# The projection's input rows cut as three tiles of 128 and a rest of 64, and the two products of u placed side by side

## Chip, cores and metric

The kernel runs on one core of one Trainium2 chip. The metric is the device time of one execution in microseconds (us); less is better. The kernel before took 781.15 us as the median of three runs (775.3 to 781.82).

## What is computed

One sequence `u` of 2048 rows and 448 channels goes through two branches, and a gate per row mixes them:

```python
g = sigmoid((x * gate_w).sum(-1, keepdims=True))
a = A(x)          # long convolution per channel by FFT, kernel K from log_A_real, A_imag, C, log_dt; plus u * D_skip
b = B(x)          # q, k, v = x @ wq, x @ wk, x @ wv; 16 heads of 28; four segments of 512 rows:
                  # causal softmax inside the segment, and a memory M, z of all earlier segments; then @ wo
return g * a + (1 - g) * b
```

The change touches the three projections `x @ wq`, `x @ wk`, `x @ wv` (448 inputs each) and the first transform of `u`'s FFT.

## The kernel before

**Split products.** q, k and v need nearly full fp32 accuracy, and the kernel gets it from single-pass products (type fp32r) of split operands: `x = xh + xl`, `w = wh + wl`, and `x w = xh wh + xh wl + xl wh`. The 448 inputs lie as four tiles of 112 partitions, so one output takes 4 x 3 = 12 products, accumulated in one PSUM bank. `matmuls` (L784) does that for a unit, that is one of 4 segments, one group of 4 heads, q or k: 12 products of 112 x 128 weights with 512 columns; there are 32 units. `values` (L857) does it for v and the gate's sum: 12 products of 450 columns for each of 16 blocks of 128 rows.

**Making the parts.** For each block of 128 rows of u, four transposes (L899) bring 4 x 112 channels onto partitions in one PSUM bank; `copy(xh, pv)` (L905) rounds them, and one subtraction on VectorE (L906) leaves `xl`. The weights of q and k are split once and stored to DRAM (`WD`, L769), 448 KB for each group of heads and matrix, and loaded again for every unit (L780, one unit ahead). The weights of v are split by `rest` (L742) and stay.

**u's transform.** `transform_u` (L541) makes the first step of u's FFT: 16 loads of u with 64 rows on the upper and 64 on the lower half of the partitions, and for each half one fp32 product of 64 rows, 128 outputs and 448 columns (each is two instructions in the trace), copied out of PSUM (`gs`) and stored (`GU`). It yields after each of the 32 products.

**The first half's order.** `first_half` (L312) makes the convolution kernel K in 56 items `n`, four to a group; each item needs three passes of ScalarE (`cs`) over 128 x 1024, four VectorE products (L409 to L415) and 64 small products on TensorE (`sums`, tile `ps_k`); between groups `decays` makes six exponentials. Into this sequence `Feed` (L493) mixes the projection, step by step: each step yields a cost, a positive or negative number of us, and `spend` (L511) gives each item an allowance, `ITEMS[n % 4] * RATES[n // 4]`, and each place in `decays` one of `PLACE`; steps are issued until the allowance is used up, what is over or short is carried on, and a negative cost ends the turn. A yield of `"pe"` after each pair of units holds the feed until the next exponentials (`exps`, L519), so that ScalarE doesn't change its table more often.

**The filler.** u's products are the filler. `project` takes two at both sides of `remember()` in its light stretches (L952, L955) and one at the start of segments 1 to 3 (L891). `spend` takes one more when the feed is held and over 1.5 us of allowance are left (L516). What is left of the 32 is issued around the last items: `fill(2)` (L477), `fill(4, False)` (L482) and `rest` (L533).

**Queues.** TensorE takes its products in the order of the program (`mm`, L1521). In the main loop ScalarE's activations and copies are chained in program order, too (`follow`, L1472). Products of projection, memory and u all write PSUM tiles `ps_m`, of which there are three (L1647). Of a pair of units both tiles are kept until the exponentials, copies and subtractions that follow the hold have read them (L960 to L967). `transform_k` (L570) and the attention follow, with other PSUM tiles and the whole of `kb`, which L436 fills after the last `sums`.

Of the kernel before, what the change touches and what calls it, by code (L numbers as in the profile page):

```python
# [12 lines left out]
F32 = mybir.dt.float32  # L13
# [298 lines left out]
def first_half(nc, k, gy, feed):  # L312
# [228 lines left out]
def transform_u(nc, k, up, pp):  # L541

    uv = k.u.rearrange("(n h w) d -> h n w d", h=2, w=16)
    guv = k.GU.rearrange("k r (h w) d -> h (k r) w d", h=2)
    def load(w):
        ut = up.tile([128, D], F32, tag="ut", name="ut", bufs=3)
        for h in range(2):
            nc.sync.dma_start(ut[64 * h : 64 * h + 64], uv[h, :, w])
        return ut

    uts = {0: load(0), 1: load(1)}
    for w in range(16):
        if w < 14:
            uts[w + 2] = load(w + 2)
        ut = uts.pop(w)
        for h in range(2):
            pt = k.ps("m")
            k.mm(
                pt[:, :D], k.s1u[64 * h : 64 * h + 64], ut[64 * h : 64 * h + 64],
                start=True, stop=True,  # L560
            )

            where, tag, bufs = (pp, "xin", 4) if w >= 12 and h else (up, "gs", 3)
            gs = where.tile([128, D], F32, tag=tag, name="gs", bufs=bufs)
            k.copy(gs, pt[:, :D], AF.Copy)
            nc.sync.dma_start(guv[h, :, w], gs)
            yield 0.9
# [156 lines left out]
def project(nc, k, pp, early, filling):  # L724

    act, copy, v = k.act, k.copy, nc.vector
    gw = pp.tile([112, 4, 2], F32, name="gw")
    nc.gpsimd.memset(gw, 0.0)
    nc.sync.dma_start(gw[:, :, 0], k.gate_w.rearrange("(k p) -> p k", p=112))
    wvh = pp.tile([112, 4, 450], F32R, name="wvh")  # L730
    wvl = pp.tile([112, 4, 450], F32R, name="wvl")
# [6 lines left out]
    nid = early.tile([112, 112], F32R, name="nid")  # L738
    with k.issue_after(k.chained):
        v.tensor_scalar(nid, k.ident[:112, :112], -1.0, None, ALU.mult)  # L740

    def rest(lo, x, hi):  # L742

        pt = k.ps("m")[:112, : x.shape[-1]]
        k.mm(pt, k.ident[:112, :112], x, start=True, stop=False)
        k.mm(pt, nid, hi, start=False, stop=True)
        copy(lo, pt, AF.Copy)

    wsp = [pp.tile([112, 4, 2, 4, 32], F32R, name=f"wsp{i}") for i in range(2)]
# [3 lines left out]
    def weights():  # L753
        for kt in range(4):
            t = pp.tile([112, D], F32, tag="xin", name="winv", bufs=4)
            nc.sync.dma_start(t, k.wv[112 * kt : 112 * kt + 112])
            for x, n in ((gw[:, kt], slice(448, 450)), (t, slice(0, D))):
                copy(wvh[:, kt, n], x, AF.Copy)
                rest(wvl[:, kt, n], x, wvh[:, kt, n])
            yield 0.3  # L760
        for i, src in enumerate((k.wq, k.wk)):
            for kt in range(4):
                t = pp.tile([112, D], F32, tag="xin", name="win", bufs=4)
                (k.bulk if i else nc.sync.dma_start)(t, src[112 * kt : 112 * kt + 112])
# [10 lines left out]
    def load_w(u):  # L775
# [3 lines left out]
        w = pp.tile([112, 4, 2, 128], F32R, tag="w", name="w", bufs=2)  # L779
# [4 lines left out]
    def matmuls(u, x):  # L784
# [3 lines left out]
        n = 0  # L788
# [68 lines left out]
    def values(s, xh, xl, ts):  # L857
        for t in ts:
            pt = k.ps("m")
            n = 0  # L860
            for kt in range(4):
                for a, b in ((xh, wvh), (xh, wvl), (xl, wvh)):
                    k.mm(
                        pt[:, :450], a[:, kt, 128 * t : 128 * t + 128], b[:, kt],
                        start=(n == 0), stop=(n == 11),
                    )
                    n += 1
                if kt == 1:
# [19 lines left out]
    for s in range(NSEG):  # L888
# [3 lines left out]
        xh = pp.tile([112, 4, SEG], F32R, tag="xh", name="xh")  # L892
        xl = pp.tile([112, 4, SEG], F32R, tag="xl", name="xl")
        for t in range(4):
# [4 lines left out]
            for kt in range(4):  # L899
                k.tr(  # L900
                    pt[:112, 128 * kt : 128 * kt + 128], xin[:, 112 * kt : 112 * kt + 112], k.ident
                )
# [3 lines left out]
            v.tensor_tensor(xl[:, :, ts_], pv, xh[:, :, ts_], ALU.subtract)  # L906
# [36 lines left out]
        for i in range(0, len(units), 2):  # L943
# [6 lines left out]
            for u in us:  # L950
                if pts:
                    for _ in range(2 if light else 0):  # L952
                        yield -next(filling, 0.1)
                    yield from remember()
                    for _ in range(2 if light else 0):  # L955
# [3 lines left out]
                yield 0.65  # L959
# [506 lines left out]
def gated_mix(ctx, tc, k):  # L1466
# [110 lines left out]
    k.WD = dr.tile([2, 4, 112, 4, 2, 128], F32, name="WD")  # L1577
# [182 lines left out]
```

## Time and profile before

| | |
|---|---|
| median of the three runs | 781.15 us |
| the profiled execution: its own time | 780.51 us |
| its span, first to last instruction | 778.7 us (1.8 us lie outside) |
| busy: TensorE (PE) / VectorE (DVE) / ScalarE (ACT) | 681.5 / 560.4 / 502.7 us |
| mean granted TensorE clock | 0.967 |
| first half (to the last `sums`) | about 0 to 419 us |
| DMA, mean over the span | 203 GB/s |

A row of the timeline gives start, duration, engine, line, operation, output <- inputs, the shape as rows*columns of the weights and the moving tile, and how many instructions are merged; in brackets stands how long the engine was idle before, and what ended that. Matmuls are pipelined: a product's duration overlaps the next one's, and what it costs on TensorE is the distance from its start to the next start. All TensorE products share one line (L1522), so they are told apart by their tiles. In a table of windows each row gives the stretch, its length, and for each engine its busy time and number of instructions, then granted clock, DMA share and GB/s. A row of a group gives count | busy time, mean ns of one | idle time before.

### The profile page before, as it was taken

Reading aid. Unit: us, or ns where it says so; the run is one execution under the profiler, and the core shown is the slowest. Engines: PE = TensorE matmul, PEld = TensorE weight load, DVE = VectorE, ACT = ScalarE, POOL = GpSimd, SP = SyncE. Lnnn points to the kernel's source line nnn. Section 1 sums busy time; section 2 is a strip of 40 time slices with the busy share of each in tenths; the row PEclk is TensorE's granted clock in tenths of the full one; section 3 lists DMA queues with packets and bytes.
Section 4 is the critical chain, followed back from the end, with each engine's and each line's share of the span. In section 5 each row is a group of like instructions: output and inputs, shape, how many; then the busy total and the mean of one; then the engine's idle time right before and its main releaser. Section 6 shows DMA issues by size and latency. Waiting matters only on the chain.

```text
span 778.7 us, 19775 instructions
## 1 busy us (share of the span) xinstructions
PE 681.5 (88%) x8273; PEld 371.0 (48%) x8289; DVE 560.4 (72%) x758; ACT 502.7 (65%) x621; POOL 157.9 (20%) x193
## 2 busy tenths in 40 slices
PE   1685998999988998889999999898899789979897
PEld 1362555666555665457664444343334334434333
DVE  8989679878899788888875345565555675674486
ACT  4877689889999989988986425665435353451220
POOL 5405300110111101110120002343311221132110
PEclk9998999999999999999999989999999899999899
DMA  9428774234563345733356797999676867556686
GB/s 242 127 71 247 231 250 131 70 106 161 156 219 111 108 126 168 231 130 105 117 211 237 283 323 274 324 333 338 230 233 207 305 208 244 195 195 242 171 266 191
DMA packets 91550, 158.00 MB, mean 203 GB/s; under 512 B 22174, under 2 KB 59542, under 8 KB 91462
## 3 DMA queue, kind: packets, MB, share of 16 engines
q1 hardware_dynamic: 85530, 153.55, 59.9%
q10 hardware_dynamic: 5052, 2.33, 1.2%
q8 instruction: 65, 1.06, 0.6%
q0 software_dynamic: 880, 0.87, 0.4%
q14 instruction: 23, 0.19, 0.1%
HBM read 88.51 MB, written 60.24 MB: 191 GB/s over the span
## 4 chain that ended last, share of the span: by engine, by line
PE 53%; ACT 18%; DVE 14%; DMA 8%; issue 4%; SPq 1%; POOL 1%; ACTq 0%; DVEq 0%; POOLq 0%
PE ps_m L1522 23%; PE ps_c L1522 8%; ACT cs L1476 6%; PE ps_w L1522 5%; PE ps_pv L1522 5%; PE ps_arg L1522 4%; PE ps_mx L1522 4%; PE ps_k L1522 4%; ACT EY L1476 2%; DVE pr L1476 2%; DVE mx L1476 2%; DMA WD<-wsp 1%; DVE xl L906 1%; ACT L1476 1%; DMA V<-VD 1%
## 5 line engine op out<-in xcount | busy, mean ns | idle before, releaser
L1476 DVE TENSOR_REDUCE mx<-ps_mx 128x2 f32<-128x1024 f32 (+3 forms) x128 | 102.4, 821 | 96.2 <-PE ps_mx L1522 93.1
L1476 ACT ACTIVATE PT<-ps_w 128x1024 f32<-128x1024 f32 (+1 forms) x96 | 84.5, 881 | 128.5 <-PE ps_w L1522 119.4
L366 POOL TENSOR_TENSOR EX<-EX,cab 128x1024 f32<-128x1024 f32 x28 | 53.5, 1913 | 288.2 <-ACT EX L1476 266.6
L1476 ACT ACTIVATE cs<-ps_arg 128x1024 f32<-128x1024 f32 x97 | 94.5, 1023 | 3.7 <-DVE Y L414 2.4
L1522 PE MATMUL ps_w<-qu,ku 32*128 32x512 f32 (+3 forms) x768 | 89.5, 350 | 4.6 <-ACT PT L1476 3.3
L1098 POOL TENSOR_SCALAR_AFFINE_SELECT PT<-PT 128x256 f32<-128x256 f32 (+1 forms) x96 | 47.4, 494 | 227.0 <-ACT PT L1476 219.6
L1522 PE MATMUL ps_m<-xh,w 112*128 112x512 f32 x256 | 91.4, 410 | 1.3 <-DMA w<-WD 1.3
L1522 PEld LDWEIGHTS ps_w<-qu,ku 32*128 32x128 f32 x768 | 58.6, 189 | 68.0 <-ACT PT L1476 30.7
L409 DVE TENSOR_TENSOR X<-EX,cs 128x1024 f32<-128x1024 f32 x56 | 69.3, 1238 | 12.6 <-ACT cs L1476 11.8
L1522 PE MATMUL ps_k<-Y,X 128*32 128x64 f32 x3584 | 64.1, 226 | 14.4 <-DVE Y L414 14.4
L1522 PEld LDWEIGHTS ps_k<-Y,X 128*32 128x32 f32 x3584 | 54.9, 113 | 40.4 <-DVE Y L414 22.4
L413 DVE TENSOR_TENSOR Y<-EY,cs 128x1024 f32<-128x1024 f32 x56 | 70.1, 1253 | 0.0
L1476 ACT ACTIVATE cs<-cs 128x1024 f32<-128x1024 f32 x56 | 59.2, 1057 | 1.3
L1522 PEld LDWEIGHTS ps_m<-xh,w 112*128 112x128 f32 x256 | 48.1, 188 | 21.1 <-issue 8.3
L1476 ACT ACTIVATE EY<-ps_arg 128x1024 f32<-128x1024 f32 x52 | 51.3, 1036 | 3.9 <-PE ps_arg L1522 3.7
L1522 PE MATMUL ps_arg<-ct,lh 64*128 64x512 bf16 x224 | 46.4, 384 | 7.0 <-ACT EY L1476 4.9
L1522 PE MATMUL ps_m<-xl,w 112*128 112x512 f32 x128 | 50.3, 393 | 0.0
L1522 PE MATMUL ps_pv<-PT,V 128*32 128x128 f32 (+3 forms) x512 | 46.4, 461 | 4.4 <-DMA V<-VD 4.4
L1522 PEld LDWEIGHTS <-lh 64*128 64x128 bf16 x392 | 20.2, 94 | 59.0 <-issue 46.5
L1522 PE MATMUL ps_m<-wo,pvs 128*128 128x448 f32 x96 | 43.9, 589 | 1.4 <-ACT mn L1476 1.1
L1522 PE MATMUL ps_mx<-ku,qu 32*128 32x512 f32 (+3 forms) x256 | 44.4, 379 | 0.3 <-DMA ku<-KD 0.3
L415 DVE SCALAR_TENSOR_TENSOR Y<-EY,cs 128x512 f32<-128x512 f32 x56 | 40.0, 715 | 3.8 <-ACT cs L1476 2.5
(219 smaller groups left out, 1284.0 us busy)
## 6 DMA issues: line engine op xcount, KB each, us to landing
w<-WD SPq DMA_DIRECT2D x32, 448.0 KB
qu<-QD SPq DMA_DIRECT2D x16, 512.0 KB
ku<-KD SPq DMA_DIRECT2D x16, 512.0 KB
GU<-gs SPq DMA_DIRECT2D x32, 224.0 KB
GK<-gs SPq DMA_DIRECT2D x8, 896.0 KB
gk<-GK SPq DMA_DIRECT2D x16, 448.0 KB
gu<-GU SPq DMA_DIRECT2D x16, 448.0 KB
ks<-ks SPq DMA_DIRECT2D x32, 224.0 KB
```

The costliest lines, as they stand in the source:

```text
L366: nc.gpsimd.tensor_tensor(o, o, cab, ALU.mult)
L409: v.tensor_tensor(X, ex, t[:, :, 0], ALU.mult)
L413: v.tensor_tensor(Y[:, :, :, :32], lo, y[:, :, :, ::-1], ALU.mult)
L415: v.scalar_tensor_tensor(Y[:, 1, :, 32:], ey[:, :, 32:], -1.0, y[:, 1], ALU.mult, ALU.mult)
L906: v.tensor_tensor(xl[:, :, ts_], pv, xh[:, :, ts_], ALU.subtract)
L1098: nc.gpsimd.affine_select(sl, sl, pat, ALU.is_ge, 0.0, base=0, channel_multiplier=-1)
L1476: x = op(*args, **kw)
L1522: tc.keep_in_program_order(nc.tensor.matmul(*args, **kw))
```

## The change

- The 448 inputs are cut as 128 + 128 + 128 + 64. The first three tiles take three products each. The fourth tile holds both parts: rows 64 to 127 the rounded channels 384 to 447, rows 0 to 63 what the rounding left of them, and the weights of these channels twice. One product of 128 rows then gives `xh wh + xl wh`, and one product of the upper 64 rows gives `xh wl`: 11 products instead of 12.
- `xl` has three tiles; the subtraction is two instructions, one of 128 x 384 and one from the upper to the lower 64 partitions of 128 columns.
- `WD` and its tiles have 128 partitions instead of 112 (512 KB a load instead of 448); the rest of each weight matrix and of `gate_w` is loaded twice, by two DMAs.
- u's two products of a load stand next to each other, with `tile_position` given; then come both copies and stores, and one yield of 1.7 instead of two of 0.9. The filler has 16 pairs instead of 32 products; `fill(1)`, `fill(2, False)` and one step instead of two in the light stretches take the same number of products at these places.
- A unit's last step costs the feed 0.45 instead of 0.65, a block of v 1.0 instead of 1.2. `RATES`, `ITEMS` and `PLACE` stay.

```diff
@@ first_half
-            feed.fill(2)
+            feed.fill(1)
...
-    feed.fill(4, False)
+    feed.fill(2, False)
@@ transform_u
-        for h in range(2):
-            pt = k.ps("m")
+        pts = [k.ps("m") for _ in range(2)]
+        for h, pt in enumerate(pts):
             k.mm(
                 pt[:, :D], k.s1u[64 * h : 64 * h + 64], ut[64 * h : 64 * h + 64],
-                start=True, stop=True,
+                start=True, stop=True, tile_position=(64 * h, 0),
             )
-
+        for h, pt in enumerate(pts):
             where, tag, bufs = (pp, "xin", 4) if w >= 12 and h else (up, "gs", 3)
             gs = where.tile([128, D], F32, tag=tag, name="gs", bufs=bufs)
             k.copy(gs, pt[:, :D], AF.Copy)
             nc.sync.dma_start(guv[h, :, w], gs)
-            yield 0.9
+        yield 1.7
@@ project
+    def terms(x, w):
+        xh, xl = x
+        wh, wl = w
+        for kt in range(3):
+            yield xh[:, kt], wh[:, kt]
+            yield xh[:, kt], wl[:, kt]
+            yield xl[:, kt], wh[:, kt]
+        yield xh[:, 3], wh[:, 3]
+        yield xh[64:, 3], wl[64:, 3]
@@ matmuls
-        for kt in range(4):
-            for a, b in ((0, 0), (0, 1), (1, 0)):
-                k.mm(pt, w[:, kt, a], x[b][:, kt], start=(n == 0), stop=(n == 11))
-                n += 1
-            if kt < 3:
+        for n, (a, b) in enumerate(terms(x, (w[:, :, 0], w[:, :, 1]))):
+            k.mm(pt, b, a, start=(n == 0), stop=(n == 10))
+            if n in (2, 5, 8):
                 yield 0.65
@@ values: the same, with n == 5 for the yield inside a block, and at its end
-            yield 1.2
+            yield 1.0
@@ the parts of x
-            for kt in range(4):
-                k.tr(
-                    pt[:112, 128 * kt : 128 * kt + 128], xin[:, 112 * kt : 112 * kt + 112], k.ident
-                )
-            pv = pt[:112].rearrange("p (k q) -> p k q", k=4)
+            for kt, c in enumerate((0, 128, 256, 320)):
+                k.tr(pt[:, 128 * kt : 128 * kt + 128], xin[:, c : c + 128], k.ident)
+            pv = pt.rearrange("p (k q) -> p k q", k=4)
             ts_ = slice(128 * t, 128 * t + 128)
             copy(xh[:, :, ts_], pv, AF.Copy)
-            v.tensor_tensor(xl[:, :, ts_], pv, xh[:, :, ts_], ALU.subtract)
+            v.tensor_tensor(xl[:, :, ts_], pv[:, :3], xh[:, :3, ts_], ALU.subtract)
+            v.tensor_tensor(xh[:64, 3, ts_], pv[64:, 3], xh[64:, 3, ts_], ALU.subtract)
@@ the units
-                    for _ in range(2 if light else 0):
+                    if light:
                         yield -next(filling, 0.1)
                     yield from remember()
-                    for _ in range(2 if light else 0):
+                    if light:
                         yield -next(filling, 0.1)
                 pts.append((yield from matmuls(u, x)))
                 load_w(after[u])
-                yield 0.65
+                yield 0.45
@@ DRAM
-    k.WD = dr.tile([2, 4, 112, 4, 2, 128], F32, name="WD")
+    k.WD = dr.tile([2, 4, 128, 4, 2, 128], F32, name="WD")
```

More of the change, by code (lines that the diff above doesn't have):

```diff
@@ L754, in weights @@
         for kt in range(4):
-            t = pp.tile([112, D], F32, tag="xin", name="winv", bufs=4)
-            nc.sync.dma_start(t, k.wv[112 * kt : 112 * kt + 112])
+            t = pp.tile([128, D], F32, tag="xin", name="winv", bufs=4)
+            rows(nc.sync.dma_start, t, k.wv, kt)
             for x, n in ((gw[:, kt], slice(448, 450)), (t, slice(0, D))):
@@ L859, in values @@
             pt = k.ps("m")
-            n = 0
-            for kt in range(4):
[L862 to L865, printed above, removed]
-                    )
-                    n += 1
-                if kt == 1:
+            for n, (a, b) in enumerate(terms((xh, xl), (wvh, wvl))):
+                k.mm(
+                    pt[:, :450], a[:, 128 * t : 128 * t + 128], b,
+                    start=(n == 0), stop=(n == 10),
+                )
+                if n == 5:
                     yield 1.2
```

39 lines of the change are left out of this document (22 added, 17 removed).

## The prediction

> **What bounds the kernel now.** I read the page first, then a table of windows cut at the first X product of each group of four items, then the timeline of single stretches, and the chain of waits last.
>
> ```profile
> span 778.7 us, 19775 instructions
> ```
>
> ```profile
> PE 53%; ACT 18%; DVE 14%; DMA 8%; issue 4%; SPq 1%; POOL 1%; ACTq 0%; DVEq 0%; POOLq 0%
> ```
>
> The chain is more than half TensorE, but everything that the change touches lies in the first half, and there the limit alternates:
>
> ```profile
> core 0: us, PE busy (x) PEld busy (x) DVE busy (x) ACT busy (x) POOL busy (x), PEclk, DMA share, GB/s
> 199.89:223.49 23.60, 21.64 (x347) 12.95 (x347) 21.73 (x29) 23.00 (x28) 3.82 (x2) 1.00 0.61 198
> 223.49:248.22 24.73, 20.78 (x354) 12.40 (x350) 23.90 (x35) 23.75 (x30) 3.83 (x2) 1.00 0.45 147
> 248.22:273.76 25.54, 25.01 (x362) 18.08 (x363) 20.86 (x30) 22.71 (x26) 3.83 (x2) 1.00 0.28 86
> 273.76:299.08 25.32, 23.91 (x353) 15.01 (x353) 21.01 (x29) 22.74 (x26) 3.82 (x2) 1.00 0.54 173
> 322.46:349.51 27.05, 23.10 (x359) 13.97 (x357) 24.25 (x33) 24.39 (x31) 3.83 (x2) 0.94 0.42 141
> ```
>
> Where v and the first units of a segment are made (248 to 299), TensorE is busy for 25.0 and 23.9 us and ScalarE idles 2.8 and 2.6 us. Where the light stretches with the filler lie (200 to 248), ScalarE is busy for 23.0 of 23.6 us, and TensorE has 2 to 4 us to spare. A TensorE saving counts in the first kind only; whatever ScalarE must do or wait for costs time in the second kind.
>
> **A unit and a block of v.** The timeline around one unit:
>
> ```profile
> 153.46 0.38 PE L1522 MATMUL ps_arg<-mag,one 64*128 64x512 bf16 x2
> ...
> 153.68 0.38 PE L1522 MATMUL ps_arg<-ct,lh 64*128 64x512 bf16 x2
> ...
> 153.99 0.50 PE L1522 MATMUL ps_m<-xh,w 112*128 112x512 f32 x1
> ...
> 154.33 0.40 PE L1522 MATMUL ps_m<-xl,w 112*128 112x512 f32 x1
> ...
> 156.42 0.39 PE L1522 MATMUL ps_m<-xl,w 112*128 112x512 f32 x1
> ...
> 156.66 0.39 PE L1522 MATMUL ps_m<-xh,w 112*128 112x512 f32 x1
> ...
> 156.97 1.10 PE L1522 MATMUL ps_k<-Y,X 128*32 128x64 f32 x64
> ```
>
> Starts inside the unit are 0.23 apart (156.42 to 156.66). Two products of 64 rows take 0.22 together (153.46 to 153.68), so one takes that long as well. A change of the rows and columns that a product occupies costs extra: 0.31 from the last 64-row pair to the unit (153.68 to 153.99, 0.09 more), 0.34 for the unit's first product (0.11 more), 0.31 for its last one before `ps_k` (0.08 more). The new unit has ten full products and a 64-row one at its end. So it saves two full products, 0.46, and pays 0.22 and one more change, 0.09: a gain of 0.15 where `ps_k` follows. Where `ps_arg` or u follows, the 64-row form is needed anyway: 0.24. Where a full product follows, the way there and back costs 0.22 + 0.08 + 0.09 + 0.11 = 0.50, a loss of 0.04. By the order of the timeline 17, 12 and 3 of the 32 units end so. For all units that is 5.3 us; about 16 of them lie where TensorE is the limit: **-2.6 us**.
>
> ```profile
> 164.66 0.37 PE L1522 MATMUL ps_m<-wvl,xh 112*128 112x450 f32 x1
> ...
> 164.87 0.37 PE L1522 MATMUL ps_m<-wvh,xl 112*128 112x450 f32 x1
> ```
>
> For v a product is 0.21. Of the twelve blocks of segments 1 to 3 seven end before `ps_arg` (gain 0.20 each), one before `ps_k` (0.11), four before a full product (loss 0.08): -1.2. The four of segment 0 end before full products: +0.3. Together **-0.9 us**.
>
> **The parts of x.** The subtraction becomes two.
>
> ```profile
> L409 DVE TENSOR_TENSOR X<-EX,cs 128x1024 f32<-128x1024 f32 x56 | 69.3, 1238 | 12.6 <-ACT cs L1476 11.8 <-DVE macc L851 0.3
> ...
> L414 DVE TENSOR_TENSOR Y<-EY,cs 128x512 f32<-128x512 f32 x56 | 39.3, 702 | 0.0
> ...
> L1476 ACT ACTIVATE gs<-ps_m 128x448 f32<-128x448 f32 x21 | 11.1, 540 | 7.0 <-PE ps_m L1522 7.0
> ...
> L906 DVE TENSOR_TENSOR xl<-ps_m,xh 112x512 fp32r<-112x512 f32 x16 | 10.3, 684 | 0.7 <-ACT xh L1476 0.7
> ```
>
> 1024 columns take 1.238, 512 take 0.702: 0.00105 a column and 0.166 fixed. At most the second instruction adds that fixed part to each of 16 subtractions, 2.7 us; at least nothing, where VectorE has room. Twelve lie in busy decays (23.90 us of 24.73): I take **+1.0**.
>
> **Weights.** Each load and store of `WD` is a seventh larger.
>
> ```profile
> 65.55 6.35 DMA WD<-wsp
> ...
> 77.90 3.97 DMA WD<-wsp
> ...
> 85.28 5.51 DMA w<-WD
> ```
>
> These 15.8 us of the chain of waits are exposed. If they grow with the bytes it is +2.3, if their time is latency 0; **+0.8**. The five extra small DMAs go through SP's queue before 60 us, under the parameters' VectorE work: 0, at most the 0.3 to 0.4 each that SP needs, 2 us.
>
> **u's pairs: where the feed puts them.** This is the term that decides. Costs fall by 0.2 per unit and block, allowances stay, so the feed reaches its hold earlier. Item 23 (allowance 2.5 x 1.12 = 2.80): before, it enters with 0.98, spends four steps of 0.65, and has 1.18 left at the hold, under the 1.5 of L516. After, item 22 already does three steps, item 23 enters with -0.57, spends 0.45, and is held with 1.78: it asks for filler. Going through all yields like this, filler in the hold is taken before at items 7 and 55 only; after at 7, 11, 19, 23, 27 and 35. So the last pair goes out at item 37, and none is left for the tail.
>
> In the hold both tiles of a pair of units are unread, and `ps_m` has three. A pair of u needs two, so the second product waits until ScalarE has copied the first out, on a queue behind the item's three `cs` passes; behind that product TensorE holds `sums` and the next exponents. Then ScalarE waits for the product. The tail of before shows such a turn:
>
> ```profile
> 416.69 0.62 DVE L1476 COPY gs<-ps_m 128x448 f32<-128x448 f32 x1
> ...
> 417.37 1.02 PE L1522 MATMUL ps_m<-ut,s1u 64*128 64x448 f32 x2 [0.31 <-DVE gs L1476]
> ...
> 418.32 1.10 PE L1522 MATMUL ps_k<-Y,X 128*32 128x64 f32 x64
> 418.47 0.54 ACT L1476 ACTIVATE gs<-ps_m 128x448 f32<-128x448 f32 x1 [0.83 <-PE ps_m L1522]
> ```
>
> The copy ends at 417.31, the product starts at 417.37, the next copy at 418.47: 1.16 us. With the copies, 2 x 0.54, ScalarE is held up 2.24 us a time. How full it is there:
>
> ```profile
> 207.88 1.94 ACT L1476 ACTIVATE cs<-ps_arg 128x1024 f32<-128x1024 f32 x2
> ...
> 209.85 1.06 ACT L1476 ACTIVATE cs<-cs 128x1024 f32<-128x1024 f32 x1
> ...
> 210.94 1.28 ACT L1476 ACT_TABLE_LOAD   x1
> ```
>
> At item 23 it goes from `cs` to the exponentials' table without a gap. Items 23 and 27 pay in full, 4.5; at 19 and 35 the same turn blocks TensorE (0.95 + 0.6 + 0.95) in groups that it limits, about 2 each; items 7 and 11 have slack, 0.5. Bounds: 0, if all lies in slack, and 6 x 2.24 = 13.4. I take **+9**.
>
> **What that frees.** The group at 322 loses three copies on ScalarE, -1.6. In the tail the product at 417.37 no longer stands ahead of the last `sums` (418.32), which sets `kb` and the second half: -1.0. Together **-2.6**. Elsewhere u's products side by side save TensorE time that is spare.
>
> **Sum.** -2.6 - 0.9 + 1.0 + 0.8 + 9 - 2.6 = +4.7 on the profiled execution's 780.5 (span 778.7 and 1.8 outside it): 785.2, rounded to **785 us**. The median of before, 781.15, is 0.6 above that execution, within its runs' spread.
>
> **Rivals.**
>
> *The waits in the hold are covered.* For it: a hold with 1.5 us left means that the item has less TensorE work than planned, and 273.76 to 299.08 shows ScalarE idle 2.6 us. Against it: no gap after 209.85. It replaces +9 by 0: **776**.
>
> *Two full products saved and no change paid, on a path that is TensorE all over.* A chain with 53% PE speaks for it: 32 x 0.23 + 16 x 0.21 = -10.7, with the pairs covered and -1.0 in the tail: **769**. Against it stand the 0.31 and 0.34 above and ScalarE's 23.00 of 23.60.
>
> *The clock falls in the new waits* (slower). With TensorE waiting behind a pair's first product, a stretch can look like the first of these:
>
> ```profile
> 133.20:136.60 3.40, 1.60 (x10) 0.59 (x7) 3.40 (x6) 3.40 (x6) 0.00 (x0) 1.00 0.73 257
> 136.60:140.00 3.40, 3.40 (x76) 3.03 (x75) 2.12 (x4) 1.77 (x3) 1.55 (x1) 0.50 0.64 202
> ...
> 228.10:231.50 3.40, 2.00 (x70) 1.20 (x66) 3.40 (x5) 3.37 (x6) 0.00 (x0) 1.00 0.42 124
> ```
>
> After 3.4 us with TensorE busy for 1.60, the granted clock is 0.50 for the next 3.4; with 2.00 busy it stayed at 1.00. That is the point from which it decides: an item with a hold and under about 1.8 us of TensorE work. A half-speed stretch does 1.7 us of work less; four of the six on the path are +6.8: **792**. [...]
>
> *The change doesn't do what it says*, if the 64-row product occupies the whole array. Then no change is paid, and each unit and block saves one full product net: for the 16 units and 16 blocks on the path 16 x 0.23 + 16 x 0.21 = 7.0 instead of my 3.5: **782**, hardly to be told from the forecast by time.
>
> **How the numbers follow.** Forecast (with the last rival) 0.50, covered waits 0.20, full saving 0.13, clock 0.17. About 1%, 7.8 us, is what a measurement of this kernel can tell from no change, that is 773 to 789. The full saving, and the lower part of the covered waits (with the subtraction and the weights at their lower bounds, 774, and the second half's order free to shift), are faster: 0.20. The clock, and the forecast with 13.4 for the waits (789.6) or both bounds of subtraction and weights, are slower: 0.32. The rest is 0.48. The range takes in the full saving at its end and the clock with the larger waits: 769 to 797. The forecast's own range is 776 to 793.
>
> **What would show it.** Right: no u product after about 370 us; in six places a `ut,s1u` pair with a `gs` copy between its two products, and ScalarE idle 0.6 to 1.2 us before the second copy; each unit 0.15 to 0.24 shorter; 0.3 around the 64-row product; last `sums` directly after its item. Wrong: the pairs in the hold start together; the groups at 200 to 248 not longer; or the second half, which the change doesn't touch, differing by more than a us or two.

## The result and the profile after

The changed kernel took **854.25 us** (median of four runs, 850.67 to 857.62) beside 781.09 for the kernel before on the same chip: a ratio of **1.095**, 95% interval 1.089 to 1.102. The forecast was 785, the range 769 to 797. A ratio below comes, like this one, from runs side by side; where disturbed runs are left out of it, it needn't be the quotient of the medians.

The profiled execution took 850.67 us, 70.2 more than that of before. The first and the last X product (items 0 and 55) cut both spans in three. The two rows are the answers for the line of the X product, before and after: count, durations, first and last start.

```profile
L409 DVE TENSOR_TENSOR X<-EX,cs x56: 1211/1221/2148, 63.0 to 413.8; 128x1024 f32<-128x1024 f32 x56
```

```profile
span 849.0 us, 19734 instructions
...
L409 DVE TENSOR_TENSOR X<-EX,cs x56: 1209/1218/2167, 65.3 to 446.0; 128x1024 f32<-128x1024 f32 x56
```

So 2.3 us are lost before item 0, 29.9 in the main loop (380.7 instead of 350.8), and **38.1 from the last X product to the end** (403.0 instead of 364.9), where nothing but the calls of the filler is changed.

**The tail and the second half.** Windows of after, then of before, with TensorE's busy time first and the granted clock third from the end:

```profile
443.53:446.94 3.41, 1.10 (x64) 0.94 (x64) 3.41 (x5) 3.36 (x4) 0.00 (x0) 1.00 0.44 160
446.94:450.36 3.42, 1.40 (x55) 1.41 (x59) 2.62 (x9) 0.39 (x3) 0.00 (x0) 0.50 0.00 0
480.00:500.00 20.00, 20.00 (x83) 8.10 (x81) 2.67 (x4) 4.58 (x5) 0.00 (x0) 0.50 0.26 107
```

```profile
412.96:416.38 3.42, 2.66 (x69) 1.80 (x70) 3.42 (x5) 2.59 (x5) 0.00 (x0) 1.00 0.47 144
416.38:419.79 3.41, 3.10 (x69) 1.53 (x68) 1.24 (x3) 1.13 (x3) 0.28 (x1) 1.00 0.85 314
```

Before, the filler of the tail keeps TensorE busy for 2.66 and 3.10 us of 3.4. With the change none is left; the `sums` alone are 1.10, and the next window runs at 0.50. It then stays there for 85 us, to 532.28, although TensorE is busy for 20.00 of 20 us in between. The timeline of that place in after:

```profile
445.48 1.10 PE L1536 MATMUL ps_k<-Y,X 128*32 128x64 f32 x64 [2.57 <-DVE Y L414]
448.96 1.93 PE L1536 MATMUL ps_k<-Y,X 128*32 128x64 f32 x64 [2.37 <-DVE Y L414]
452.13 3.36 PE L1536 MATMUL ps_w<-kb,s1k 32*128 32x448 f32 x8 [1.24 <-DVE kb L436]
```

Eight products of `transform_k` take 3.36 us; before they take 1.77 (at 420.68). So the products do run at the clock that the records show. The window before the fall wasn't idle: TensorE was busy for 1.10 of its 3.41 us. Nor did a busy TensorE bring the full clock back: from 452 to 529 us the distances between starts give about 62 us to products of 32 rows and 13 to products of 128, with 2.0 us of gaps, and the clock stayed at 0.50.

**The main loop.** TensorE's waits between 90 and 410 us, us in total, times, longest; after, then before:

```profile
PE ps_m L1539 <- DMA xin<-in_A_u: 3.9, 2, 2.3
PE ps_m L1536 <- ACT gs L1490: 3.8, 6, 0.6
PE ps_m L1536 <- DVE tm L872: 3.6, 3, 1.2
...
PE ps_m L1536 <- DVE lo L827: 2.3, 2, 2.1
PE ps_m L1536 <- DVE lo L829: 2.2, 1, 2.2
```

```profile
PE ps_m L1522 <- DVE macc L851: 0.4, 1, 0.4
```

Waits for `gs`, `tm` and `lo` are new, 11.9 us, and 11.7 of them stand ahead of products of u, which wait for a reader of a `ps_m` tile. New are also 3.9 us in which the transposes wait for the load of `xin`. One place of the first kind in after, a pair in the hold and the next one in the decay behind it:

```profile
251.85 1.02 PE L1536 MATMUL ps_m<-ut,s1u 64*128 64x448 f32 x2
...
252.90 0.54 ACT L1490 ACTIVATE gs<-ps_m 128x448 f32<-128x448 f32 x1 [2.65 <-PE ps_m L1536]
...
253.50 1.02 PE L1536 MATMUL ps_m<-ut,s1u 64*128 64x448 f32 x2 [0.63 <-ACT gs L1490]
...
254.55 0.55 ACT L1490 ACTIVATE gs<-ps_m 128x448 f32<-128x448 f32 x1 [1.11 <-PE ps_m L1536]
...
255.92 0.91 PE L1536 MATMUL ps_m<-ut,s1u 64*128 64x448 f32 x2
...
258.92 0.85 PE L1536 MATMUL ps_m<-ut,s1u 64*128 64x448 f32 x1 [2.08 <-DVE lo L827]
```

The first four rows are the turn that the prediction worked out. The last two aren't in it: the pair at 255.92, outside of the hold, needs its second tile while the units still keep theirs, and waits for VectorE's `lo`.

### The profile page after: what moved, and what is told of

The parts are those of the page before. It is cut to its first block, busy times and chain, and to the rows that moved or that the text cites. A ratio compares the mean times of both kernels' runs of the same rounds, so it can differ in the third digit from the quotient of the medians.

```text
span 849.0 us, 19734 instructions
## 1 busy us (share of the span) xinstructions
PE 727.8 (86%) x8224; PEld 377.3 (44%) x8241; DVE 566.7 (67%) x775; ACT 503.2 (59%) x620; POOL 156.4 (18%) x193
## 4 chain that ended last, share of the span: by engine, by line
PE 46%; DVE 14%; ACT 11%; DMA 7%; issue 3%; SPq 1%; DVEq 0%; ACTq 0%; POOL 0%
PE ps_m L1536 17%; PE ps_c L1536 8%; PE ps_w L1536 6%; PE ps_pv L1536 5%; PE ps_mx L1536 4%; PE ps_k L1536 3%; PE ps_arg L1536 3%; ACT cs L1490 2%; DMA ks<-ks 2%; DVE pr L1490 2%; DVE Y L413 2%; ACT L1490 2%; DVE X L409 1%; DVE pvs L1490 1%; ACT EY L1490 1%
## 5 line engine op out<-in xcount | busy, mean ns | idle before, releaser
L1536 PE MATMUL ps_w<-qu,ku 32*128 32x512 f32 (+3 forms) x768 | 91.7, 357 | 4.3 <-ACT PT L1490 3.9
L1536 PE MATMUL ps_m<-xh,w 128*128 128x512 f32 (+1 forms) x256 | 92.8, 433 | 1.6 <-DMA w<-WD 1.6
L1536 PEld LDWEIGHTS ps_w<-qu,ku 32*128 32x128 f32 x768 | 60.5, 195 | 67.8 <-ACT PT L1490 31.5
L1536 PE MATMUL ps_k<-Y,X 128*32 128x64 f32 x3584 | 68.5, 234 | 14.2 <-DVE Y L414 13.9
L409 DVE TENSOR_TENSOR X<-EX,cs 128x1024 f32<-128x1024 f32 x56 | 69.3, 1237 | 14.6 <-ACT cs L1490 12.5
L1536 PEld LDWEIGHTS ps_k<-Y,X 128*32 128x32 f32 x3584 | 58.7, 119 | 38.6 <-DVE Y L414 18.2
L1536 PEld LDWEIGHTS ps_m<-xh,w 128*128 128x128 f32 (+1 forms) x256 | 45.3, 189 | 32.6 <-issue 20.3
L1536 PE MATMUL ps_arg<-ce,lh 64*128 64x512 bf16 x168 | 36.5, 403 | 14.1 <-ACT EY L1490 8.3
L1536 PE MATMUL ps_mx<-ku,qu 32*128 32x512 f32 (+3 forms) x256 | 47.7, 405 | 0.0
L1536 PEld LDWEIGHTS <-lh 64*128 64x128 bf16 x392 | 22.1, 95 | 55.5 <-issue 44.6
```

The source lines that it names most:

```text
L409: v.tensor_tensor(X, ex, t[:, :, 0], ALU.mult)
L1536: tc.keep_in_program_order(nc.tensor.matmul(*args, **kw))
```

## The experiments

The table gives each kernel's profiled execution in the three parts, and the ratio to before. Half clock is the time at 0.50, in us, of the stretches that begin between 72 us and the last X product.

| kernel | first X | to last X | last X to end | half clock | ratio |
|---|---|---|---|---|---|
| before | 63.0 | 350.8 | 364.9 | 7 | 1 |
| after | 65.3 | 380.7 | 403.0 | 31 | 1.095 |
| e2 work in the tail | 66.1 | 378.7 | 361.3 | 27 | 1.041 |
| e4 before, filler early | 63.6 | 359.1 | 390.5 | 7 | 1.053 |
| e1 no takes in holds | 65.4 | 383.1 | 397.7 | 44 | 1.088 |
| e5 old costs | 65.4 | 386.5 | 401.4 | 44 | 1.088 |
| e6 pairs alone | 63.8 | 369.6 | 399.5 | 17 | 1.066 |
| e8 projection alone, old costs | 66.9 | 358.1 | 367.6 | 14 | 1.019 |
| e7 projection alone, new costs | 66.3 | 372.3 | 396.1 | 20 | 1.073 |
| e11 the same, no takes in holds | 66.2 | 357.2 | 403.9 | 14 | 1.062 |
| e18 e8 with low rows | 66.6 | 350.9 | 371.7 | 7 | 1.012 |

**Theories.** A: the feed takes u's products too early; the takes in the hold slow the first half, and the empty tail costs the clock. Rivals: B, the second half is slower for a reason of its own; C, the new projection (the products of 11, the subtractions or the weights) slows the first half; A2, formed after e1, a pair costs time wherever it needs two of three `ps_m` tiles; D, two products side by side cost time as such.

### The tail: e2 and e4

e2 is after with products in place of the filler, e4 is before without filler in the tail.

```diff
+        if n >= 2 * NJ - 2:
+            k.turn_over(k.ps("m"), 8)
...
     sums(2 * NJ - 1)
+    k.turn_over(k.ps("m"), 4)
```

> The changed kernel, with 8 + 8 + 4 bf16 products of 128 x 512 on unused ps_m tiles after the sums of the last items, where the filler was before; the order of u's pairs is unchanged. The products compute nothing that is used. Theory A: the first half is as slow as in the changed kernel (last X product at 444 to 448), the clock stays at 1.00 after it, and from there to the end it is 363 to 370 us: 810 to 820 in all. Rival B: the second half stays at about 400 us, 850 or more in all.

Measured: 812.73 us, 41.5 less than after; 361.3 us from the last X product to the end, 2 under what A gave. Where after waited, e2 has:

```profile
447.78 1.10 PE L1539 MATMUL ps_k<-Y,X 128*32 128x64 f32 x64 [0.54 <-DVE Y L414]
448.81 1.04 PE L1539 MATMUL ps_m<-ct,one 128*128 128x512 bf16 x4
450.15 1.77 PE L1539 MATMUL ps_w<-kb,s1k 32*128 32x448 f32 x8 [0.30 <-DVE kb L436]
```

```diff
         product(n)
+        if 44 <= n < 53:
+            feed.fill(1)
```

> The kernel before, with nothing of the change; its last nine u products are issued one each at items 44 to 52, so that none is left for the tail. Theory A: the tail's gaps halve the clock near the last item and it stays at 0.50 through the transform of K; the second half takes about 400 us instead of 365, 815 to 825 in all. Rival B: the clock holds, 781 to 787.

Measured: 819.79 us, ratio 1.053 (1.044 to 1.062). Without a line of the change the clock falls at 423.71 and stays at 0.50 for 85 us (the mean granted clock, 0.926 over a span of 813.2 us, comes to 120 us at 0.50 in all), and the products of `transform_k` take 3.36:

```profile
428.81 3.36 PE L1524 MATMUL ps_w<-kb,s1k 32*128 32x448 f32 x8 [1.23 <-DVE kb L436]
```

B falls: e2 has the whole change and no slower second half, e4 has nothing of the change and the slower one. 25.6 us (e4 against before) to 41.7 us (e2 against after) behind the last X product hang on what TensorE does in three gaps of 1.2 to 2.6 us. That e4 loses less than the 38.1 of the change comes mostly from later falls of the clock: behind the long stretch it has 21 us more at 0.50, after has 37, and half of the difference is an estimated 8 of the 12.5. Nor is filler free where it goes early: nine single products at items 44 to 52 cost e4's main loop 8.3 us.

### The feed: e1, e5, e7, e11

e1 is after with one number changed; e11 is the same edit with u's single products.

```diff
-        if self.due > 1.5 and (self.held or self.done) and self.waiting:
+        if self.due > 99.0 and (self.held or self.done) and self.waiting:
```

> The changed kernel, but the filler is never taken in a hold; by the feed's own accounts 16 pairs then go to 13 planned places and 3 pairs (6 products) are left for the last items. Theory A (the pairs taken in the hold cost the first half its 32 us, and the empty tail lets the clock fall and costs the second half its 38 us): the last X product starts at 412 to 420 us, from there to the end about 365 us, clock 1.00 through the transform of K; 776 to 790 in all. Rival B (the second half is slower for a reason of its own in the change): from the last X product to the end still about 400 us, 812 to 825 in all. Rival C (the products of 11 with their changes of mode slow the first half themselves): last X product at 435 or later.

Measured: 849.8 us, last X product at 448.6: a miss for A in both halves, and by its bound (435 or later) what C foretold; e6 and e8 below tell the pairs from the projection. And three pairs in the tail don't carry the clock: side by side, the two products of a pair take 1.02 us, what one alone takes (the prediction's row at 417.37). A pair in e1's tail, and its windows:

```profile
445.44 1.02 PE L1536 MATMUL ps_m<-ut,s1u 64*128 64x448 f32 x4
```

```profile
446.37:449.79 3.42, 1.80 (x70) 1.43 (x69) 3.42 (x5) 3.37 (x5) 0.00 (x0) 1.00 0.49 181
449.79:453.20 3.41, 2.05 (x8) 0.49 (x5) 3.41 (x9) 1.01 (x3) 0.53 (x1) 1.00 0.40 138
453.20:456.60 3.40, 2.23 (x67) 1.99 (x68) 1.95 (x5) 0.00 (x0) 1.39 (x1) 0.50 0.83 274
```

e5 is after with the feed's old costs:

```diff
-                yield 0.45
+                yield 0.65
...
-            yield 1.0
+            yield 1.2
```

> The changed kernel with the feed's costs of before (0.65 for a unit's last step, 1.2 for a block of v). By the feed's accounts a hold takes a pair at items 7 and 55 only, 14 pairs are used up by item 41 and 2 remain: one at item 55, one right after it, none ahead of the last sums. Theory A: the first half is within 5 us of before (last X product at 410 to 419). Whether two pairs carry the clock is open: 772 to 785 if they do, about 38 more if not. Rival C (the 11 products themselves): last X product at 435 or later.

Measured: 847.25, last X product at 452.0, clock lost in the tail (0.893 in the mean, before 0.967): again a miss for A, and within C's bound. The lower costs alone aren't it either.

e7 is after with `transform_u` and the numbers of fillers as before:

```diff
-        pts = [k.ps("m") for _ in range(2)]
...
+            pt = k.ps("m")
...
-        yield 1.7
...
+            yield 0.9
```

> The changed kernel with u's 32 single products instead of 16 pairs; the feed's new costs (0.45, 1.0) stay. By the feed's accounts nine single products are taken in holds before item 44 and none is left for the tail. Theory A2: a single product needs one tile, so the first half is as before within 6 us (last X product at 408 to 420); the tail is empty, the clock falls and the second half takes 398 to 405: 808 to 825 in all. If the takes in the hold cost time by themselves, as predicted, the last X product comes at 425 or later.

Measured: 836.99 us, last X product at 438.5, clock lost in the tail (0.910 in the mean). By the expectation's bound (425 or later) the takes in the hold cost time by themselves; e11 takes them out.

> The changed projection and the feed's new costs with u's 32 single products, none taken in a hold; nine are left for the tail. With holds this kernel had its last X product at 438.5 us, with the old costs at 424.9. If the takes in the hold cost the difference: 421 to 428, clock 1.00 in the tail, 786 to 798 in all. If the lower costs themselves cost it: 434 to 440, 800 to 810.

Measured: last X product at 423.4 as expected, so the takes in the hold cost e7 15 us of the main loop (372.3 against 357.2). But it took 829.0 in all, not 786 to 798: in spite of nine products in the tail the clock was lost. The last two of them (one row of the timeline of e11) waited for the load of u, and the clock fell at 430.50:

```profile
430.25 2.67 PE L1536 MATMUL ps_m<-ut,s1u 64*128 64x448 f32 x4 [1.78 <-DMA ut<-in_A_u]
```

### The two parts: e6 and e8

e6 is before with the change's `transform_u`, `fill(1)`, `fill(2, False)` and single steps in the light stretches, and nothing else; e8 is e7 with e5's edit, that is the rest of the change on the feed's old order.

> The kernel before with u's pairs alone: 12 products of 112 rows, the feed's costs of before, 16 pairs. The feed's order of pairs is that of the changed kernel with old costs. Theory A2: last X product at 440 to 452 us, the clock falls in the tail since two pairs are left for it, 840 to 858 in all. Rival C: the first half like before, last X product at 411 to 420, 775 to 825 in all by the clock.

> The projection's part of the change alone (tiles of 128 rows, 11 products, two subtractions, larger weight loads), with u's 32 single products and the feed's costs of before, so the feed's order is that of before. Theory A2, formed after the run without holds (the pairs cost the first half its time wherever they stand, because a pair needs two of the three ps_m tiles at once): last X product at 408 to 416 us, second half 365, 773 to 783 in all. Rival C (the 11 products, the subtractions or the weights slow the first half): last X product at 425 or later, 795 or more in all.

Measured: e6 833.99 us with its last X product at 433.4, e8 795.34 with its last at 424.9. The pairs alone cost the main loop 18.8 us, with every unit as before, and the clock in the tail (0.903 in the mean); that lies between what A2 (440 or later) and C (420 or earlier) foretold. The projection alone costs 7.3 and a late start: e8 stands at C's bounds (425 and 795), and A2 was too hopeful by 12 us. So both parts slow the first half.

### The pairs' tiles: e3, e9, e16, e17

e3 is after with one ring for all copies:

```diff
-            where, tag, bufs = (pp, "xin", 4) if w >= 12 and h else (up, "gs", 3)
-            gs = where.tile([128, D], F32, tag=tag, name="gs", bufs=bufs)
+            gs = up.tile([128, D], F32, tag="gs", name="gs", bufs=3)
```

> The changed kernel, with the copies of the last four pairs in the ring gs of the transform instead of the ring xin, from which the projection's loads of u also come. In the changed kernel these loads of segment 2 are issued only at 261 and 264 us and the group of items 24 to 27 takes 37.8 us, 13 more than before. If the late loads carry that, the group takes 25 to 30 us and the time falls by 7 to 12; if the pairs' waits for tiles carry it, the group stays at 32 or more and the time falls by under 5.

Measured in one run: the group takes 30.5 us, between the two forecasts, and the time is 846.58, 7.7 under after's median but only 4.1 under its profiled execution. The late `xin` loads are some 5 to 7 us of that group, which took 37.8 in after and 35.1 in e2, where the order is the same.

e9 and e16 are e6 with the pairs issued at the blocks of v and none in holds or between units; e16 without e9's ends of turns:

```diff
+            if s > 0:
+                next(filling, None)
             yield 1.2
```

> The kernel before with u's pairs alone, as in the run of the pairs, but the filler is taken after each block of v of segments 1 to 3, where no unit's tile is kept, instead of between a pair of units, and not in holds. Theory A2 (a pair needs two of three ps_m tiles while units keep theirs): TensorE's idle time ahead of u's products falls from 34.7 us to under 10, the last X product comes at 412 to 424 us instead of 433; the tail has a pair or two, so the clock falls there and the whole takes 812 to 826. Rival D (two products side by side cost time wherever they stand): idle ahead of them over 25 us, last X product at 430 or later.

Measured: 830.23 us, last X product at 419.0, but this says little: the added ends of turns left so much of the projection over that `transform_k` began at 467.6. The run decides nothing.

> The kernel before with u's pairs alone, one pair ahead of the yield after each block of v of segments 1 to 3 and one at the start of these segments, none in holds or between a pair of units; one is left for the tail. Theory A2: TensorE waits under 3 us ahead of u's products before the last items (11.6 in the run of the pairs), last X product at 413 to 424 us instead of 433; the clock falls in the tail and the whole takes 808 to 824. Rival D (a pair costs time wherever it stands): 8 us of such waits or more, last X product at 428 or later.

Measured: 841.37 us, last X product at 441.4, 7.6 us of waits ahead of u's products (11.3 in e6). A2 in this form falls, and D's bounds are met or nearly so. By the program there is no place where the tiles are free, since v, the transposes and the units use the same three. But the waits ahead of pairs fell while the main loop grew by 8.6 us: the `sums` wait 16.3 us for VectorE's `Y` there, 5.5 in e6. So the run says little on the pairs alone.

e17 is e6 with the pair in the two banks of one `ps_arg` tile (shown against e6):

```diff
-        pts = [k.ps("m") for _ in range(2)]
+        both = k.ps("arg")
+        pts = [both[:, 0], both[:, 1]]
```

> The kernel before with u's pairs alone, in the order of the run of the pairs, but the pair writes the two banks of one ps_arg tile instead of two ps_m tiles. Theory A2 (the ring ps_m is what the pairs wait for): TensorE's waits ahead of u's products for lo, tm and macc go away, at most 4 to 7 us of waits for the exponents' tiles come in their place, the last X product comes at 415 to 427 us instead of 433; the tail is short of filler as there, 810 to 828 in all. Rival D (the pair as such): last X product at 430 or later, 832 or more in all.

Measured: 833.52 us, last X product at 427.7, main loop 363.5 instead of e6's 369.6. Waits of e17 between 90 and 410 us, then of e6:

```profile
PE ps_arg L1523 <- ACT EY L1477: 14.6, 13, 2.8
...
PE ps_arg L1523 <- ACT cs L1477: 3.5, 6, 0.7
```

```profile
PE ps_arg L1522 <- ACT EY L1476: 8.6, 14, 1.3
PE ps_m L1522 <- ACT gs L1476: 6.2, 3, 3.3
...
PE ps_m L1522 <- DVE tm L854: 2.7, 4, 0.8
PE ps_m L1522 <- DVE lo L809: 2.0, 1, 2.0
```

The waits for `tm` and `lo` are gone, as A2 says, but those for the exponents' tiles grew by 9 (`cs` from 0.5), more than A2's 4 to 7; the last X product lies between A2's bound (427) and D's (430), and the total is D's. The wait moves with the pair from one ring to the other; ahead of single products there is little of it (0.4 us for 24 of them in e8, 3.9 in e11). That the two banks taken at once are the cause, and not the two products as such, fits this but isn't shown: D isn't excluded, and a pair in one bank was not tried.

### The projection: e10, e13, e14, e15, e18, e19

e10 is before with its subtraction cut in two, e13 before with split loads:

```diff
-            v.tensor_tensor(xl[:, :, ts_], pv, xh[:, :, ts_], ALU.subtract)
+            v.tensor_tensor(xl[:, :3, ts_], pv[:, :3], xh[:, :3, ts_], ALU.subtract)
+            v.tensor_tensor(xl[:, 3, ts_], pv[:, 3], xh[:, 3, ts_], ALU.subtract)
```

> The kernel before, with its subtraction for xl as two instructions of 384 and 128 columns, as many rows and the same values. In the run of the projection alone the chain on VectorE between the copy of kb and the next cs grew by 1.3 us for four blocks, and TensorE's gap behind it halved the clock twice (257 and 360 us). If this is what slowed the main loop by 7 us there: last X product 3 to 8 us later than before, 784 to 790 in all. If the predicted +1.0 holds: 781 to 783.

Measured: 782.41 us, ratio 1.002 (0.998 to 1.005): two instructions cost nothing that can be measured. So it isn't their number.

```diff
+                queue(t[56 * h : 56 * h + 56], src[336 + 56 * h : 392 + 56 * h])
```

> The kernel before, with the fourth tile of each of the three weight matrices loaded by two DMAs of 56 rows instead of one of 112: the number of DMAs of the change, without its larger tiles. In all kernels with the changed projection the first X product starts at 65.1 to 66.9 us, in those with the old one at 63.0 to 63.8. If the number of DMAs delays it: 65 or later here; if not: 63.0 to 63.9.

Measured in one run: first X product at 63.8. By this run it isn't the number of weight loads.

e14 and e18 change the rows of the second subtraction of e8 (e14 `64:`, e18 `:64` throughout); both leave out `xl wh` of the last 64 channels:

```diff
-            v.tensor_tensor(xh[:64, 3, ts_], pv[64:, 3], xh[64:, 3, ts_], ALU.subtract)
+            v.tensor_tensor(xl[:64, 3, ts_], pv[:64, 3], xh[:64, 3, ts_], ALU.subtract)
```

> The projection's part alone with the old costs, but the second subtraction writes rows 64 to 127, those that it reads, instead of rows 0 to 63; so the products lack xl wh for the last 64 channels. With the move a block takes VectorE 0.90 us there (0.55 and 0.29, with gaps), two instructions without a move took 0.67, one 0.60. If the move is what slowed the main loop: 0.67 to 0.70 for a block, from the first to the last X product 351 to 354 us instead of 358, clock 1.00 near 257 and 360 us; 785 to 791 in all. If not: 356 to 359, 793 to 798.

Measured: 795.39 us, a block still 0.88, main loop 360.3. Not the move.

> The projection's part alone with the old costs, but the second subtraction reads and writes rows 0 to 63 (so the products lack xl wh for the last 64 channels). Traces so far: with a second subtraction that reads from row 64 on, VectorE begins it only as the first ends (0.56 after its start for 0.55 us) and a block takes 0.89 us; with both from row 0 on, the second began 0.47 after the first, and a block took 0.67. If the starting row is what costs: 0.65 to 0.69 a block here, from the first to the last X product 352 to 356 us instead of 358, 787 to 793 in all. If the number of rows costs: 0.86 to 0.90 a block and 792 to 798. [...]

Measured: 791.25 us, and the main loop is **350.9, that of before** (350.8). VectorE in e8, then in e18:

```profile
248.06 0.55 DVE L919 TENSOR_TENSOR xl<-ps_m,xh 128x384 fp32r<-128x384 f32 x1
248.62 0.29 DVE L920 TENSOR_TENSOR xh<-ps_m,xh 64x128 fp32r<-64x128 f32 x1
248.95 0.56 DVE L919 TENSOR_TENSOR xl<-ps_m,xh 128x384 fp32r<-128x384 f32 x1
```

```profile
244.86 0.56 DVE L919 TENSOR_TENSOR xl<-ps_m,xh 128x384 fp32r<-128x384 f32 x1
245.33 0.27 DVE L920 TENSOR_TENSOR xl<-ps_m,xh 64x128 fp32r<-64x128 f32 x1
245.52 0.54 DVE L919 TENSOR_TENSOR xl<-ps_m,xh 128x384 fp32r<-128x384 f32 x1
```

A block takes 0.89 with the second subtraction at row 64 and 0.66 with it at row 0: at row 64 each begins only when the one before has ended. Why the starting row does this, no run shows. The group of items 24 to 27, with four such blocks in its decay, takes 26.0 us instead of 24.7 (25.0 in e18), and in e8 the gap that this leaves TensorE takes the clock, too:

```profile
253.94:257.36 3.42, 1.46 (x11) 0.86 (x11) 2.62 (x4) 3.15 (x4) 0.00 (x0) 1.00 0.27 92
257.36:260.77 3.41, 3.41 (x13) 3.11 (x12) 3.41 (x6) 2.19 (x3) 0.00 (x0) 0.50 0.00 0
```

e15 tests the late start on e8, e19 computes the whole result with e18's rows:

```diff
-        nc.sync.dma_start(gw[64 * h : 64 * h + 64, 3, 0], k.gate_w[384:])
+        nc.gpsimd.dma_start(gw[64 * h : 64 * h + 64, 3, 0], k.gate_w[384:])
```

> The projection's part alone with the old costs, but the two added loads of gate_w go through GpSimd's queue instead of SP's. In the changed kernel they take SP's queue from 9.54 to 11.67, and the first load of xin is issued at 11.71 instead of 9.14. If they cause the late start: first xin load at 9 to 9.6, first X product at 62.8 to 64.2 instead of 66.9, 790 to 793 in all. If not: 65 or later.

Measured: 795.58 us; the first `xin` load is at 9.56, the first X product at 68.3. Not the gate loads.

```diff
+                k.mm(
+                    pt[64 * h : 64 * h + 64, 384:], xin[:, 384:], k.ident,
+                    start=True, stop=True, tile_position=(0, 64 * h),
+                )
...
+            v.tensor_tensor(xh[:64, 3, ts_], pv[:64, 3], xh[:64, 3, ts_], ALU.subtract)
```

> The projection's part alone with the old costs and the whole result, but the last 64 channels are transposed twice, to rows 0 to 63 and to rows 64 to 127, so that the second subtraction reads and writes rows 0 to 63. It costs one more small product for each block of 128 rows. If the starting row was the whole price in the main loop, a block of subtractions takes 0.65 to 0.69 us and the first to the last X product 350 to 354 us, as with the low rows; the late start (65 to 67 us) stays: 783 to 792 in all, 0 to 11 more than before. Faster than before by over 1% only if the saved products count after all, which no run so far shows.

Measured: ratio 1.007 (1.002 to 1.011). A block of subtractions takes 0.67 again (253.67 to 254.34), but the main loop took 356.5 in this execution, a miss; the groups of items 0 to 7 carry 4.0 of the 5.6 us to e18, and why stays open. Without these two groups the starting row shows in all five kernels: from item 8 to the last, before and e18 take 293.4 us and e19 295.0, but e15, e8 and e14, which start at row 64, take 297.7, 298.8 and 299.8. So the row is worth some 3 to 6 us there; the rest of e8's 7.3 lies in the first groups, which vary from kernel to kernel. e18 stays 1.2% behind before for its late start and for 6.8 us behind the last X product, where its clock is at 0.50 for 47 us instead of 38; half of the difference, an estimated 4.6, is lost clock, the rest stays open. No version of the change beats the kernel before.

## Why the prediction was wrong

- **"What that frees" is the step that failed.** It priced the empty tail at -1.0, since no u product would stand ahead of the last `sums`. The order was right (the last u product starts at 335.0), but those products were all that TensorE had there. The price was the clock: +38.1 us here, and 41.7 and 25.6 in the two runs that undo it and make it (e2 and e4). The prediction's own sign of being wrong, a second half that differs by more than a us or two, came true.
- **The clock rival** stood in the prediction for the waits in holds, with 0.17 and +6.8. The mechanism was right, its place incomplete and its size too small: the point from which it decides was worked out, but not put to the tail, where `sums` of 1.1 us stand alone in an item of 3.5. Nor was the half clock expected to last. In the main loop it came true, too: 31 us at 0.50 instead of 7, and by the prediction's count, half of such time lost, that is an estimated 12 us of the 29.9.
- **"Where the feed puts them":** the takes and their turn are as worked out (the rows at 251.85 to 254.55). Their price of +9 is of the right order (e7 against e11: 15 for single products). But "that is the term that decides" is wrong twice. Pairs taken outside of holds wait as well (e6: 18.8 us without the new costs), since a step with two `ps_m` tiles waits for v's, the memory's and the units' readers; and w >= 12 takes the ring of `xin`, some 5 to 7 us in one group. So a pair was wrongly costed as two single products, and +9 is half of what e6 shows for the pairs alone.
- **The products of 11** were mis-sized. Where `ps_arg` follows, the 64-row product does run beside its first product (in after they start at 434.117, as the second product of the row at 433.80 below, and at 434.123), which so comes 0.45 us earlier; the prediction had 0.24. But the gain doesn't last. Before, the six products of 64 rows behind the unit start two at a time (402.42, 402.64, 402.86). With the change the first of them starts with the unit's last product, and the six start at 434.12, 434.35, 434.45 to 434.57, 434.68 and 434.89. From the tenth product of the unit to the next full product it is 1.53 us before (401.64, one product ahead of the first row below, to 403.17) and 1.40 after (433.80 to 435.20). Between before and e18, which has the same order, seven of eleven such places gain 0.11 to 0.15 us, the others are disturbed by waits or by a missing record.

```profile
401.87 0.39 PE L1522 MATMUL ps_m<-xl,w 112*128 112x512 f32 x1
...
402.42 0.39 PE L1522 MATMUL ps_arg<-ct,lh 64*128 64x512 bf16 x2
...
403.17 0.51 PE L1522 MATMUL ps_m<-xh,w 112*128 112x512 f32 x1
```

```profile
433.80 0.81 PE L1536 MATMUL ps_m<-xh,w 128*128 128x512 f32 x2
434.12 0.39 PE L1536 MATMUL ps_arg<-ct,lh 64*128 64x512 bf16 x1
434.35 0.38 PE L1536 MATMUL ps_arg<-mag,one 64*128 64x512 bf16 x1
...
435.20 0.73 PE L1536 MATMUL ps_m<-xh,w 128*128 128x512 f32 x2
```

  Where `ps_k` follows, the 64-row product costs 0.32 ahead and 0.43 behind, and a unit saves 0.03 instead of 0.15 (the first row below merges the last full product, at 250.07, with the 64-row one, which the second row shows alone):

```profile
250.07 0.82 PE L1536 MATMUL ps_m<-xh,w 128*128 128x512 f32 x2
...
250.39 0.50 PE L1536 MATMUL ps_m<-xh,w 64*128 64x512 f32 x1
...
250.82 1.10 PE L1536 MATMUL ps_k<-Y,X 128*32 128x64 f32 x64
```

  With 0.46 for the one unit that u follows and a loss of 0.06 where a full product follows, the units save an estimated 11 x 0.13 + 0.46 + 17 x 0.03 - 3 x 0.06 = 2.2 us in all instead of 5.3, and less where TensorE is the limit. None of it is seen: with the subtractions at row 0 (e18) the main loop is that of before.

- **The subtractions:** +1.0 was mis-sized, and the bound of 2.7, too. The second one's starting row costs the projection's main loop 7 us in e8 against e18, and 3 to 6 from item 8 on over the five kernels, part of it as lost clock. The prediction counted a fixed part for each instruction and no wait between two of them.
- **Weights and loads:** the start is 2.3 us later (2.0 to 5.4 in the other runs with the changed projection), against +0.8. One link is seen: VectorE's chain of parameters waits for `pin_cr`, which ScalarE begins at 40.95 instead of 37.20, behind a table load and the first exponents (before, then after):

```profile
37.20 1.05 ACT L277 ACTIVATE pin_cr<-pin_cr 112x1024 f32<-112x1024 f32 x1
```

```profile
37.83 1.28 ACT L1499 ACT_TABLE_LOAD   x1
...
40.95 1.06 ACT L277 ACTIVATE pin_cr<-pin_cr 112x1024 f32<-112x1024 f32 x1
```

What puts it there stays open, and the order alone isn't the whole cause: in e10 `pin_cr` stands behind the table load, too, at 38.47, and the first X product starts at 62.4. The number of weight loads (e13, one run), the gate's loads (e15) and the starting row (e18) are excluded.

The losses don't add up to the whole by parts (e6 and e8 give 18.8 + 7.3 = 26.1 of the main loop's 29.9): which waits fall on the path, and which windows lose the clock, changes from kernel to kernel.

## What to carry to other kernels

Work that fills gaps on TensorE was worth the clock that it held here, 25.6 to 41.7 us behind the last X product, not the time that it took: before making filler faster or taking it earlier, look at the stretch that is left with none, and at what runs right behind it. A step that takes two tiles of a ring of three is not two steps that take one (10.9 us of waits for `gs`, `tm` and `lo` in e6, none in before). When a schedule is balanced by costs, changing the costs moves everything that the schedule places.

## What the runs showed beyond that

- Busy time alone didn't decide the clock: a window with 1.80 us of TensorE work was followed by 1.00 and one with 2.05 by 0.50 (both in e1). But in before and after, from 72 us to 10 us behind the last X product, the windows of 3.41 us at full clock part clearly: with 1.07 to 1.39 us of TensorE work all 4 were followed by 0.50, from 1.61 to 2.36 us 6 of 22, above that none of 174. In e4 and e8 windows with 1.10, 1.14, 1.36 and 1.46 were followed by 0.50, too.
- The half clock outlasted full work: 85.33 us in after, though TensorE was busy without a gap from 457.18 to 515.00, and 85 us in e4.
- A subtraction that reads from row 64 on didn't overlap the one ahead of it, which starts at row 0: 0.56 from start to start for 0.55 us of work (e8), 0.47 for 0.56 when both start at row 0 (e18).
- In after a single product of 64 rows and another one of 64 rows start side by side (0.006 us apart, at 434.12), but the pairs behind them are broken up, so that 0.13 of the 0.45 us is left. Between a full one and `ps_k` it took 0.75 (250.07 to 250.82), three times a full product's 0.23.
